# Six warm-up matmuls taken out of the tail of an attention and MLP kernel

## The chip, the cores and the metric

The kernel runs on one core of one Trainium2 chip. The metric is the device time of one execution in microseconds (us). All executions quoted were marked as fast, none as slow. The profiles give the span between the first and the last instruction, which is 1.7 to 1.9 us shorter than the device time in most runs.

A line of a profile gives the start, the length, the engine, the line of the kernel, the operation and its tiles; "x8" is the number of instructions merged in it, and the brackets give the idle time before it and what ended it. PE is TensorE's matmuls (and stands for TensorE in the recorded texts), PEld its weight loads, DVE VectorE, ACT ScalarE, POOL GpSimd. To evacuate a bank is to copy a finished result out of the accumulators; the kernel then sends the copy to memory.

## The reference, cut to what matters

The result is the sum of a normalized input's attention, a token-mixing MLP and the input itself:

```python
x = A_x                                   # [1, 2048, 512], bf16
xn = _layernorm(x, axis=-1)
return x + _A_ref(xn, A_wqkv, A_wo) + _B_ref(xn, B_w1, B_b1, B_w2, B_b2)
# _A_ref: 32 heads of 16, softmax over 2048 keys, heads joined, then "@ wo"
```

What matters here is the last step for the last quarter of the rows: all heads' results times `wo`, plus a part that has been computed earlier.

## The kernel before

The kernel is a program that lays out every instruction in order when it is built. Scores, exponentials and the products with V fill the first 675 us. The tail then projects the last heads for four tiles of 128 rows. `oT` holds the heads in four groups, T = 0 to 3. Groups 0 and 1 are long in the accumulators. Group 2 and a half of group 3 come from earlier blocks. The other half of group 3, `oL`, is what the very last block leaves, and VectorE has to normalize it first.

```python
def warm_up(n, bk, src=pT[:, NPB - 1, 0:512], keys=(("pT", NPB - 1),)):
    for _ in range(n):          # a result that nobody reads: keeps TensorE busy
        sc.add("pe", lambda e: e.matmul(bank(bk), lhsT=src[:, 0:128], rhs=src, start=True, stop=True),
               reads=keys, writes=[("bank", bk)], cost=("F", (0, 1, 2, 3), 0.3), name="warm")

def task_last():                # VectorE: normalize the last block
    ...                         # cut: views
    yield op(lambda e: e.transpose(denb[:, tb_, :], bank(PV_BANK)), ...)        # L1121
    yield op(lambda e: e.reciprocal(rcomp[:, 0, :], ...), ...)                  # L1123
    for half in range(2):
        yield op(lambda e, half=half: e.transpose(..., rl[:, :, half, :]...), ...)                          # L1127
        yield op(lambda e, half=half: e.tensor_tensor(v(oL, half), v(bank(PV_BANK), half), ..., ALU.mult),  # L1130
                 ..., [("oTl", half)], ...)

def tail():
    ...                         # cut: which banks
    def heads_of(Tm, sti):      # L1142: one 128x512 matmul for row tile sti
        ...
    for sti in range(4):
        heads_of(2, sti)
    warm_up(6, 2 * slots[1] + 1, wo_c[:, 0, :], wk)
    for sti in range(4):
        heads_of(3, sti)        # waits for L1095 on VectorE
    for half in range(2):       # L1155: eight matmuls, four on each half of oL
        for sti in (half, half + 2):
            for a in range(2):
                ...             # lhsT=oL[...half...], rhs=wo_t[...], reads ("oTl", half)
    for sti in (0, 2, 1, 3):    # evacuate: ScalarE for tile 3, VectorE for the others
        ...                     # L1162 (ScalarE), L1165 (VectorE), then one output transfer each
```

The softmax here doesn't subtract the row's maximum and nothing guards it: scores larger than these inputs give would overflow.

Of the kernel before, what the change touches and what calls it, by code (L numbers as in the profile page):

```python
# [359 lines left out]
def bass_parallel_sum__softmax_full_mha__mixer_token_mlp__prompt_kernel(  # L360
# [18 lines left out]
    with ExitStack() as es:  # L379
        block = es.enter_context(nc.Block())  # L380

        def sb(name, shape, dt):
            return es.enter_context(nc.sbuf_tensor(name, shape, dt))
# [14 lines left out]
        wo_c = sb("wo_c", [128, 4, D], BF16)  # L398
# [18 lines left out]
        def oT(qb):  # L417
            return oT_a[:, qb] if qb < 2 else oT_b[:, qb - 2]
# [23 lines left out]
        def bank(i):  # L442
            return ps[:, i * 512:(i + 1) * 512]
# [6 lines left out]
        def dma(q, dst, src, reads, writes, name="", noncontig=False, out_dma=False, cost=None):  # L450
            if noncontig:
                def fn(eng, dst=dst, src=src):
                    with nc.allow_non_contiguous_dma(reason="tiny strided vector load"):
                        return eng.dma_start(dst, src)
            else:
                def fn(eng, dst=dst, src=src):
                    return eng.dma_start(dst, src)
            return sc.add(q, fn, reads=reads, writes=writes, name=name, dma=True, out_dma=out_dma, cost=cost)
# [208 lines left out]
        def warm_up(n, bk, src=pT[:, NPB - 1, 0:512], keys=(("pT", NPB - 1),)):  # L667
            for _ in range(n):
                sc.add("pe", lambda e: e.matmul(bank(bk), lhsT=src[:, 0:128], rhs=src, start=True, stop=True),  # L669
                       reads=keys, writes=[("bank", bk)], cost=("F", (0, 1, 2, 3), 0.3), name="warm")  # L670
# [463 lines left out]
        def tail():  # L1134
            qb, T = NQB - 1, 3
            wk = [("wo_c", e_, r) for e_ in range(2) for r in range(4)]
            slots = sorted(range(3), key=lambda z: sc.ready("pe", [], [("bank", 2 * z), ("bank", 2 * z + 1)]))
            tbk = [2 * slots[0], 2 * slots[0] + 1, 2 * slots[1], EX_BANK]
            osl = [osb[:, 0, :], osb[:, 1, :], t_bf[:, 512:1024], t_bf[:, 1024:1536]]

            def heads_of(Tm, sti):
                sc.add("pe", lambda e: e.matmul(  # L1142
                    bank(tbk[sti]), lhsT=oT(qb)[:, Tm, 128 * sti:128 * (sti + 1)], rhs=wo_c[:, Tm, :],
                    start=Tm == 2 and sti < 3, stop=False),
                    reads=[("oTc", qb, 2) if Tm == 2 else ("oTh", sti // 2)] + wk, writes=[("bank", tbk[sti])])
            for sti in range(4):
                heads_of(2, sti)
            warm_up(6, 2 * slots[1] + 1, wo_c[:, 0, :], wk)
            for sti in range(4):
                heads_of(3, sti)  # L1150
            for half in range(2):
                for sti in (half, half + 2):
                    h = sti // 2
                    for a in range(2):
                        sc.add("pe", lambda e, sti=sti, h=h, a=a, half=half: e.matmul(  # L1155
                            bank(tbk[sti]), lhsT=oL[:, 256 * a + 128 * half:256 * a + 128 * half + 128],
                            rhs=wo_t[:, 2 * h + a, :], start=False, stop=a == 1),
                            reads=[("oTl", half)] + [("wo_t", c) for c in range(4)], writes=[("bank", tbk[sti])])
            for sti in (0, 2, 1, 3):
                st = 4 * qb + sti  # L1160
                if sti == 3:
                    sc.add("act", lambda e: e.activation(osl[3], bank(tbk[3]), ACTF.Identity),  # L1162
                           reads=[("bank", tbk[3])], writes=[("osl", 3)], cost=(0.5, 0.6))
                else:
                    sc.add("dve", lambda e, sti=sti: e.scalar_tensor_tensor(  # L1165
                        osl[sti], bank(tbk[sti]), 1.0, resid[:, sti, :], ALU.mult, ALU.add),
                        reads=[("bank", tbk[sti]), ("resid", sti)],
                        writes=[("osl", sti), ("osb", sti) if sti < 2 else ("osl2",)])
                dma("act" if sti == 3 else "sp", out2[128 * st:128 * (st + 1), :], osl[sti], reads=[("osl", sti)],
                    writes=[("out", st)], name="st_out", out_dma=True)  # L1170
# [467 lines left out]
        assert sorted(resid_done) == [0, 1, 2, 3]  # L1638
        load_lib(library_config.standard)
        tail()  # L1640
        if DEBUG_SCHED:
            print("modelled end", {e: round(sc.free[e], 1) for e in sc.free}, "busy", {e: round(v, 1) for e, v in sc.busy.items()},
# [54 lines left out]
```

## Time and profile before

| | before |
|---|---|
| time, median of the first 3 executions (6 in all) | 685.25 us (685.16 us) |
| span of the profiled execution | 683.2 us |
| last PV matmuls of the loop | to about 675.0 us |
| tail, from there to the end | 8 us |
| work of TensorE in the tail | 4 + 6 + 4 + 8 matmuls |

Everything that decides lies in the last 8 us, and the prediction below shows the lines. Three things have to be kept in mind in reading them. A matmul of 128x512 is recorded as 379 ns long, but the next one starts 216 ns after it (the six warm-ups of before, from 675.85 to 677.15). A VectorE instruction can start before the record of the one ahead of it ends: in the prediction's view L1127 starts at 677.02, 0.08 us before the end of L1130 (676.68 + 0.42). And a few matmul records are missing (the page of before counts 12975 matmuls and 12978 weight loads): a group shown as "x3" or "x7" can have had four or eight, and the number of weight loads tells.

### The profile page before, as it was taken

The page shows a single profiled execution, that of the slowest core. Times are in us where ns is not written, and L with a number is a line of the kernel's source. Part 1 is how long each engine was busy: PE and PEld are TensorE (multiplying, and loading weights), DVE is VectorE, ACT ScalarE, POOL GpSimd, SP SyncE. Part 2 cuts the span into 40 slices and gives each one's busy share as a digit, 9 for nine tenths or more (in the row PEclk, how much of TensorE's full clock was granted, in tenths as well). Part 3 has the DMA queues.
Part 4 walks back from the last instruction along what each step waited for, and adds up shares of the span by engine and source line. Part 5 has one row for each costly group of instructions (what it writes and reads, how often), then busy time and mean ns, then how long its engine had stood idle before and what let it go on. Part 6 is the DMA issues. An engine that isn't in the chain of part 4 may idle for free.

```text
span 683.2 us, 29532 instructions
## 1 busy us (share of the span) xinstructions
PE 671.5 (98%) x12975; PEld 312.9 (46%) x12978; DVE 617.0 (90%) x882; ACT 667.7 (98%) x731; POOL 416.7 (61%) x717
## 2 busy tenths in 40 slices
PE   8999999999999999999999999999999999999997
PEld 4534544445444455444444444444444444444443
DVE  7989899899998898999899899999999999989886
ACT  6999999999999999999999999999999999999995
POOL 5446557476576654667666677666657576565552
PEclk9999999999999999999999999999999999999999
DMA  7502100220002201122211112222221222212221
GB/s 216 132 8 52 24 15 23 51 48 24 19 18 49 49 22 20 26 49 47 49 38 27 41 44 58 53 57 47 46 59 35 59 55 56 54 45 66 46 50 46
DMA packets 86256, 32.85 MB, mean 48 GB/s; under 512 B 67440, under 2 KB 86128, under 8 KB 86128
## 3 DMA queue, kind: packets, MB, share of 16 engines
q1 hardware_dynamic: 85696, 30.58, 19.8%
q8 instruction: 101, 1.65, 1.0%
q10 hardware_dynamic: 432, 0.39, 0.2%
q14 instruction: 27, 0.22, 0.1%
HBM read 21.76 MB, written 2.35 MB: 35 GB/s over the span
## 4 chain that ended last, share of the span: by engine, by line
PE 73%; ACT 21%; DVE 3%; issue 1%; POOL 1%; DVEq 0%
PE ps L843 29%; PE ps L776 27%; PE ps L874 14%; ACT pT L800 14%; ACT x_sb L800 6%; PE ps L928 2%; ACT gT_sb L985 1%; DVE hx L588 1%; DVE pT L811 1%; POOL mv L584 0%; PE ps L669 0%; DVE x_sb L811 0%; PE ps L600 0%; PE ps L1155 0%; PE ps L1142 0%
## 5 line engine op out<-in xcount | busy, mean ns | idle before, releaser
L800 ACT ACTIVATE pT<-ps 128x1024 bf16<-128x1024 f32 x488 | 486.4, 1136 | 2.2 <-PE ps L776 1.7
L811 DVE TENSOR_SCALAR pT<-ps 128x1024 int16<-128x1024 f32 x220 | 269.2, 1224 | 26.2 <-PE ps L776 17.4
L776 PE MATMUL ps<-QT,KT 32*128 32x512 bf16 x2048 | 283.3, 384 | 5.3 <-ACT pT L800 3.2
L817 POOL INT64_ADD pT<-pT x342 | 206.5, 613 | 121.4 <-DVE pT L820 57.2
L843 PE MATMUL ps<-pT,V 128*32 128x256 bf16 x4696 | 242.1, 275 | 0.9 <-POOL pT L817 0.3
L800 ACT ACTIVATE x_sb<-ps 128x1024 bf16<-128x1024 f32 x223 | 241.7, 1142 | 0.2
L776 PEld LDWEIGHTS ps<-QT,KT 32*128 32x128 bf16 x2048 | 78.3, 91 | 179.7 <-ACT pT L800 66.9
L843 PEld LDWEIGHTS ps<-pT,V 128*32 128x32 bf16 x4696 | 111.7, 96 | 69.2 <-issue 55.3
L811 DVE TENSOR_SCALAR x_sb<-ps 128x1024 int16<-128x1024 f32 x93 | 113.7, 1222 | 9.7 <-PE ps L776 6.9
L817 POOL INT64_ADD pT<-x_sb x152 | 91.5, 612 | 48.8 <-DVE pT L820 28.8
L843 PE MATMUL ps<-x_sb,V 128*32 128x256 bf16 x1904 | 120.8, 275 | 0.0
L817 POOL INT64_ADD x_sb<-pT x120 | 73.1, 613 | 45.0 <-DVE pT L820 26.1
L843 PE MATMUL ps<-pT,VM 128*32 128x256 bf16 x920 | 63.7, 275 | 0.0
L820 DVE TENSOR_SCALAR pT<-pT 128x1024 int16<-128x1024 int16 x138 | 58.3, 425 | 3.9
L843 PEld LDWEIGHTS ps<-x_sb,V 128*32 128x32 bf16 x1904 | 49.5, 96 | 25.0 <-issue 20.8
L874 PE MATMUL ps<-gT_sb,wblk 128*32 128x512 bf16 (+1 forms) x704 | 57.9, 384 | 0.0
L874 PE MATMUL ps<-hx,wblk 128*32 128x512 bf16 x598 | 52.5, 383 | 0.1
L817 POOL INT64_ADD x_sb<-x_sb x44 | 26.9, 614 | 18.1 <-DVE pT L820 11.7
L882 PE MATMUL ps<-hx,wblk 32*128 32x512 bf16 (+1 forms) x92 | 35.5, 386 | 0.0
L843 PEld LDWEIGHTS ps<-pT,VM 128*32 128x32 bf16 x920 | 24.2, 96 | 12.8 <-issue 12.2
L820 DVE TENSOR_SCALAR pT<-x_sb 128x1024 int16<-128x1024 int16 x64 | 27.0, 425 | 1.9
L820 DVE TENSOR_SCALAR x_sb<-pT 128x1024 int16<-128x1024 int16 x60 | 25.6, 428 | 1.7
(107 smaller groups left out, 444.2 us busy)
## 6 DMA issues: line engine op xcount, KB each, us to landing
wblk<-in_B_w_dram SPq DMA_DIRECT2D x10, 512.0 KB, 4.3
wblk<-in_B_w_dram SPq DMA_DIRECT2D x16, 320.0 KB, 3.7
oC<-OT SPq DMA_DIRECT2D x248, 16.0 KB, 1.8
denb<-rden_scratch SPq DMA_DIRECT2D x124, 32.0 KB, 2.0
xr<-in_A_x_dram SPq DMA_DIRECT2D x16, 128.0 KB, 2.8
dcomp<-OT SPq DMA_DIRECT2D x124, 2.0 KB, 1.8
QT<-Qall SPq DMA_DIRECT2D x120, 16.0 KB, 1.8
out_dram<-osb SPq DMA_DIRECT2D x14, 128.0 KB, 1.9
```

Of the source, the lines that this page charges most:

```text
L588: return [dict(eng="dve", fn=lambda e: e.tensor_scalar(xn_sb[:, t, :], xn_sb[:, t, :], mv[:, t, 3:4], None, ALU.mult), reads=[("xn", t), ( ...
L776: specs.append(dict(eng="pe", fn=lambda e, r=r, bk=bk: e.matmul(bank(bk), lhsT=KT[32 * r:32 * r + 32, T, 128 * kt:128 * (kt + 1)], rhs=QT[ ...
L800: return [dict(eng="act", fn=lambda e: e.activation(buf(pbuf[n]), ps[:, s_ * 1024:(s_ + 1) * 1024], ACTF.Exp, scale=LN2_128), reads=[("ban ...
L811: return dict(eng="dve", fn=lambda e: e.tensor_scalar(buf_i(w), ps[:, s_ * 1024:(s_ + 1) * 1024], IBIAS, 0.0, ALU.add, ALU.max), reads=[(" ...
L817: return dict(eng=eng, fn=lambda e: e.int64_add(buf_i(o).bitcast(I64), buf_i(w).bitcast(I64), SHIFTS[k] * 0x0001000100010001), reads=[("pT ...
L820: return dict(eng=eng, fn=lambda e: e.tensor_scalar(buf_i(o), buf_i(w), float(SHIFTS[k]), 1.0, ALU.add, ALU.mult), reads=[("pT", w)], writ ...
L843: specs.append(dict(eng="pe", fn=lambda e, c=c, h=h, i=i, off=off: e.matmul(bank(PV_BANK)[32 * c:32 * c + 32, 256 * par:256 * par + 256], ...
L874: specs.append(dict(eng="pe", fn=lambda e, c=c, w=w: e.matmul(bank(EX_BANK)[32 * c:32 * c + w, :], lhsT=lhs_of(32 * c, 32 * c + w), rhs=rh ...
L882: return [dict(eng="pe", fn=lambda e: e.matmul(bank(EX_BANK)[0:dst_rows, :], lhsT=lhs_of(0, dst_rows)[rs], rhs=rhs[rs], start=begin, stop= ...
L928: return [dict(eng="pe", fn=lambda e, ct=ct, c=c: e.matmul(bank(EX_BANK)[32 * c:32 * c + 32, 128 * i:128 * (i + 1)], lhsT=xnT[:, ct, 128 * ...
L985: yield "act", [dict(eng="act", fn=lambda e, ap=ap: e.activation(ap, ap, ACTF.Gelu_apprx_tanh), reads=[("gT", f) for f in fts], writes=[(" ...
```

## The change

The intent: nobody reads the six warm-ups' results. They only keep TensorE busy while VectorE prepares the last heads; that this was meant to hold its clock is my reading of it. (In the profile of before the granted clock is 1.00 up to 682.0 us and 0.50 to 0.51 from there on, with TensorE's last matmul started at 679.52.) The four matmuls of group 3 can fill that wait as well, and they are needed anyway.

```diff
@@ -1145,7 +1145,6 @@
             for sti in range(4):
                 heads_of(2, sti)
-            warm_up(6, 2 * slots[1] + 1, wo_c[:, 0, :], wk)
             for sti in range(4):
                 heads_of(3, sti)
```

Lines below it are numbered one lower afterwards: L1155 becomes L1154, L1162 L1161 and L1165 L1164.

## The prediction

Cuts are marked in the text below: what they said of the hardware is not shown by any run of this case. No term of the sum is among them. The 0.216 us for each matmul is read from the six warm-ups in the profile of before, and the sum came to a gain of 0.80 to 0.84 us, taken as 0.81: 685.25 - 0.81 = 684.44 us. Step 3's 0.2155 us is 0.2158 us in that profile, (679.521 - 678.010) / 7, and the last start comes to 678.68 with either.

> **What bounds the kernel now.** I looked first at the page's summary, the engines' busy shares, to see whether six matmuls could matter at all.

> ```profile
> PE 671.5 (98%) x12975; PEld 312.9 (46%) x12978; DVE 617.0 (90%) x882; ACT 667.7 (98%) x731; POOL 416.7 (61%) x717
> ```

> TensorE and ScalarE are both busy for 98% of the span. But these are averages over 683.2 us, and the edited line runs once, in the last 8 us. Nothing ahead of it moves: the kernel is a list of instructions laid out in order when it is built, and the call that goes is the last part of that list but one. The banks of the tail are picked before it. So the whole question lies in the window from 674 us to the end, and its own limits decide. Second view: the chain of waits that ended last, for that window.

> ```profile
> 673.95 1.09 PE ps L843 x40
> 675.04 0.16 issue
> 675.20 0.81 PE ps L1142 x3
> 676.01 1.29 PE ps L669 x6
> 677.31 0.86 PE ps L1142 x4
> 678.17 1.74 PE ps L1155 x8
> 679.91 0.02 issue
> 679.94 0.60 ACT oT L1162
> ```

> The columns are start, length, and what ran. The six warm-up matmuls (L669) lie on the chain for 1.29 us, between the projection of the heads of T = 2 (L1142, first group) and that of T = 3 (L1142, second group), and the eight matmuls of the very last heads (L1155) close it. The first L1142 group shows three matmuls, where the code has four. Four weight loads are there, the first at 674.97, so I take the record of the first matmul as missing: it ran at about 674.98 and the "issue" of 0.16 us isn't a real wait. PE is then gapless from 674.98 to the start of the last matmul.

> On a chain does not yet mean worth its length. Third view: the timeline of VectorE in the same window, which makes what L1155 reads (columns: start, length, what; in brackets the idle time before it).

> ```profile
> 674.38 0.87 DVE L1095 TENSOR_TENSOR wkv_raw<-oC,denb 64x256 bf16<-64x256 f32 x2 [1.82 <-DMA oC<-OT]
> 675.17 0.70 DVE L1121 STREAM_TRANSPOSE denb<-ps 128x512 f32<-128x512 f32 x1
> 675.91 0.25 DVE L1123 RECIPROCAL rcomp<-denb 128x16 f32<-128x16 f32 x1
> 676.20 0.45 DVE L1127 STREAM_TRANSPOSE oC<-rcomp 128x256 f32<-128x256 f32 x1
> 676.68 0.42 DVE L1130 TENSOR_TENSOR oT<-ps,oC 128x256 bf16<-128x256 f32 x1
> 677.02 0.44 DVE L1127 STREAM_TRANSPOSE oC<-rcomp 128x256 f32<-128x256 f32 x1
> 677.49 0.43 DVE L1130 TENSOR_TENSOR oT<-ps,oC 128x256 bf16<-128x256 f32 x1
> 678.64 0.69 DVE L1165 SCALAR_TENSOR_TENSOR osb<-ps,hx 128x512 bf16<-128x512 f32 x1 [0.73 <-PE ps L1155]
> 679.25 0.68 DVE L1165 SCALAR_TENSOR_TENSOR oT<-ps,hx 128x512 bf16<-128x512 f32 x1
> 679.85 0.68 DVE L1165 SCALAR_TENSOR_TENSOR osb<-ps,hx 128x512 bf16<-128x512 f32 x1
> ```

> Three dates are in it. The heads of T = 3 (L1095) are whole at 675.25. The first half of the very last heads (first L1130) is ready at 676.68 + 0.42 = 677.10, the second half at 677.49 + 0.43 = 677.92. L1155 starts on the first half only at 678.01, some 0.9 us after it was ready, and VectorE then idles 0.73 us for PE. So the filler is longer than the wait that it fills, and PE is the late one here.

> [...]six warm-ups from 675.85 to 677.15 are 0.216 us each, though each is recorded as 379 ns long. The recorded length is therefore not what one matmul costs.[...]

> [...]In this trace the granted clock is 1.00 in every 0.5 us stretch up to 682.0 and 0.51 from 682.0 to 682.5, with the last matmul started at 679.52. The drop thus came some 2.1 us after PE had run out of work (679.9)[...], and it fell when nothing needed PE any more.

> **The change, part by part.** Removed: six 128x512 matmuls, 6 x 0.216 = 1.30 us of PE. Nothing is added, and no wait goes, since the bank that they wrote belongs to the slot whose other bank the projection takes anyway, and nobody read theirs.

> Moved, step by step:
> 1. The four matmuls of T = 2 end their issue at 675.85, as now. Those of T = 3 follow at once, because their data is whole at 675.25: they start at 675.85 instead of 677.15 and hold PE to 675.85 + 4 x 0.216 = 676.71.
> 2. L1155 then waits for the first half: ready at 677.10, plus the way from VectorE to PE. I read that from one case where PE stood idle for VectorE: the copy of the last but one block ends at 659.95 and the next weight load is at 660.01, so 0.06 us. The first matmul starts at about 677.17 instead of 678.01. PE is idle for 677.17 - 676.71 = 0.46 us. The gain on PE is 0.84 us, not 1.30.
> 3. Four matmuls on the first half run to 677.17 + 0.86 = 678.03. The second half is seen by PE at 677.92 + 0.06 = 677.98, so just in time. The last matmul starts at 677.17 + 7 x 0.2155 = 678.68 (now 679.52).
> 4. Evacuation on VectorE. From the start of a bank's last matmul to its evacuation it is now 678.64 - 678.23 = 0.41 us. The first bank is complete for it at 677.17 + 0.22 + 0.41 = 677.80, but VectorE works on the second L1130. From a TENSOR_TENSOR of this shape to the next instruction it is 677.02 - 676.68 = 0.34 us, so it is free at 677.83. VectorE is now the later one, by 0.03 us. Three evacuations at the present spacing of 0.605 us start at 677.83, 678.44 and 679.04 (their banks are complete at 677.80, 678.23 and 678.66). The last starts at 679.04 instead of 679.85: 0.81 us earlier.
> 5. Evacuation on ScalarE (L1162) follows the last matmul: 678.68 + 0.42 = 679.10 instead of 679.94: 0.84 us earlier.
> 6. Four output transfers follow at the same spacing as now, two of them issued last and together (680.56 now, from both queues), 1.8 to 2.1 us to land. They can only shift. The later of the two issues moves by 0.80 us.

> Sum: 0.80 to 0.84 us, limited by VectorE; I take 0.81. 685.25 - 0.81 = 684.44 us, 0.12% of the whole. Of the 1.30 us removed, 0.46 us turn into a wait for VectorE, and 0.03 us of the rest are lost to it at the evacuation.

> **The rivals.**
> - *The whole 1.30 us is gained* (683.95 us). The chain, taken at its word, says so. Against it stands the 677.10 of the first L1130: L1155 can't start before its operand exists.
> - *VectorE sets the end already, so nothing is gained* (685.2 us). For it: VectorE's line from 674.38 to 677.92 has no gap above 0.1 us, and its next work is the evacuation. Against: the 0.73 us in which it waits for L1155. This wait is the upper limit of what VectorE can give, together with the overlap of 0.08 us between two of its instructions, which is where the 0.81 comes from.
> - *The idle PE is throttled, which is what the filler was there to prevent.* If the last eight matmuls ran at half clock from 677.17, at 0.43 us each, the last would start at 680.18, 0.66 us later than now: about 685.9 us. For it: the clock does fall at the end of this very trace. Against: that took 2.1 us of idle time, and the new gap is 0.46 us behind a stretch that was full; in the loop, PE's weight loads wait hundreds of times for 0.2 to 0.4 us and the clock stays at 1.00. I give this 3%.
> - *A wait met with an empty PE queue costs more than 0.06 us.* [...]With 0.3 us the gain would be about 0.6 us (684.65 us). Each 0.1 us here, above the 0.03 us of slack in step 4, costs 0.1 us. This is the likeliest way to be off.
> - *The output transfers hide it.* No: each is issued by what its evacuation releases, 0.03 us after its end, and the first now starts at 679.36, behind everything else.

> **Range and chances.** The three runs of before lie within 0.16 us, so noise is of the order of 0.1 to 0.2 us. The mechanism leaves 0.55 to 0.9 us of gain. That gives 684.15 to 684.85 us for 8 times in 10, a little lopsided to the slow side because of the fourth rival. A change of 2% would be 13.7 us; the whole tail from the last attention block to the end is 8 us. No rival comes near, so "within 2%" is as good as certain, and the rest is for a run that is disturbed.

> **What would show it.** In the changed kernel's timeline: no L669 after the loop's own; the second L1142 group at about 675.85 in place of 677.15; an idle PE of about 0.46 us ahead of L1155 that ends by DVE oT L1130, and L1155 from about 677.17; no wait of 0.73 us ahead of the first L1165, which starts back to back with the second L1130 near 677.83; ScalarE's L1162 near 679.10; a span of about 682.4 us; granted clock 1.00 until PE is done. Wrong would be: L1155 starting later than 677.3 (the empty queue costs more), 0.43 us between matmuls (throttle), L1165 still waiting for PE by more than 0.1 us, or any shift ahead of 674 us larger than 0.1 us, which would mean that the two traces differ by something that I took as fixed.

## The result, and the profile after

The changed kernel takes 684.34 us (median of 6, 684.26 to 684.46) against 685.16 us before (median of 6, 685.07 to 685.25): 0.82 us less. The slowest run after is faster than the fastest before. The ratio is 0.9988, with a 95% interval from 0.9975 to 1.0001. Ratios here are the mean time of one kernel's fast runs over that of the other's of the same rounds, so not quite the ratio of the medians quoted. The predicted time was 684.44 us.

The order of instructions on the other four engines is the same in both kernels, and on TensorE it differs by the six matmuls alone. The page's first line after:

```profile
PE 670.7 (98%) x12969; PEld 312.4 (46%) x12972; DVE 617.0 (90%) x882; ACT 667.7 (98%) x731; POOL 417.6 (61%) x717
```

TensorE has six matmuls and six weight loads fewer. The timeline of VectorE after, to be laid beside that of before:

```profile
674.26 0.87 DVE L1095 TENSOR_TENSOR wkv_raw<-oC,denb 64x256 bf16<-64x256 f32 x2 [1.45 <-DMA oC<-OT]
675.36 0.72 DVE L1121 STREAM_TRANSPOSE denb<-ps 128x512 f32<-128x512 f32 x1 [0.23 <-PE ps L843]
...
676.88 0.42 DVE L1130 TENSOR_TENSOR oT<-ps,oC 128x256 bf16<-128x256 f32 x1
...
677.69 0.42 DVE L1130 TENSOR_TENSOR oT<-ps,oC 128x256 bf16<-128x256 f32 x1
678.03 0.68 DVE L1164 SCALAR_TENSOR_TENSOR osb<-ps,hx 128x512 bf16<-128x512 f32 x1
678.63 0.68 DVE L1164 SCALAR_TENSOR_TENSOR oT<-ps,hx 128x512 bf16<-128x512 f32 x1
679.23 0.68 DVE L1164 SCALAR_TENSOR_TENSOR osb<-ps,hx 128x512 bf16<-128x512 f32 x1
```

The wait of 0.73 us ahead of the first evacuation is gone. VectorE goes from the second L1130 straight to it, 678.03 - 677.69 = 0.34 us later. ScalarE's evacuation after:

```profile
679.30 0.60 ACT L1161 ACTIVATE oT<-ps 128x512 bf16<-128x512 f32 x1 [4.55 <-PE ps L1154]
```

The weight loads and matmuls of TensorE in the same stretch (two views of the same kernel, the weight loads first):

```profile
675.24 1.41 PEld L1142 LDWEIGHTS ps<-wo_c,wkv_raw 128*128 128x128 bf16 x8 [0.21 <-issue]
677.36 0.55 PEld L1154 LDWEIGHTS ps<-wo_t,oT 128*128 128x128 bf16 x4 [0.71 <-DVE oT L1130]
678.17 0.60 PEld L1154 LDWEIGHTS ps<-wo_t,oT 128*128 128x128 bf16 x4 [0.27 <-DVE oT L1130]
```

```profile
675.47 1.67 PE L1142 MATMUL ps<-wo_c,wkv_raw 128*128 128x512 bf16 x7 [0.16 <-issue]
677.36 1.90 PE L1154 MATMUL ps<-wo_t,oT 128*128 128x512 bf16 x8 [0.22 <-DVE oT L1130]
```

All eight L1142 run in one stretch, and the array then waits for VectorE. The wait that the view shows, 0.22 us, starts at the recorded end of the last L1142 (675.47 + 1.67 = 677.14). Counted from when the array could have taken the next matmul it is longer: the first L1142 ran at about 675.25, eight of them take 8 x 0.216 = 1.73 us, and from 676.98 to 677.36 it is 0.38 us. It differs between executions: counted in the same way, it is 0.56 us in `n0` below, which is the same kernel.

The two profiles can't be subtracted as they stand. The execution after runs late from the start: already at 102 us a given VectorE instruction (L811) is at 102.37 instead of 102.11, and it keeps this 0.26 us to the tail. So the tails are compared from a mark of their own. From the start of L1121 to the start of the last evacuation on VectorE it was 679.85 - 675.17 = 4.68 us and is 679.23 - 675.36 = 3.87 us: 0.81 us less. This quantity, "VectorE's path", is used below. It leaves out the offset, but not all of the jitter: L1121 starts 0.12 to 0.34 us after TensorE's first weight load of the tail, depending on the execution, and where TensorE sets the end, a late L1121 makes the path look shorter.

### The profile page after: what moved, and what is told of

The parts are those of the page before. It is cut to its first block, busy times and chain, and to the rows that moved or that the text cites. A ratio compares the mean times of both kernels' runs of the same rounds, so it can differ in the third digit from the quotient of the medians.

```text
span 682.6 us, 29520 instructions
## 1 busy us (share of the span) xinstructions
PE 670.7 (98%) x12969; PEld 312.4 (46%) x12972; DVE 617.0 (90%) x882; ACT 667.7 (98%) x731; POOL 417.6 (61%) x717
## 4 chain that ended last, share of the span: by engine, by line
PE 74%; ACT 21%; DVE 3%; issue 1%; POOL 1%; DVEq 0%
PE ps L843 29%; PE ps L776 27%; PE ps L874 14%; ACT pT L800 14%; ACT x_sb L800 6%; PE ps L928 2%; PE ps L669 1%; ACT gT_sb L985 1%; DVE hx L588 1%; DVE pT L811 1%; POOL mv L584 0%; PE ps L600 0%; DVE x_sb L811 0%; PE ps L613 0%; PE ps L882 0%
## 5 line engine op out<-in xcount | busy, mean ns | idle before, releaser
L811 DVE TENSOR_SCALAR pT<-ps 128x1024 int16<-128x1024 f32 x220 | 269.1, 1223 | 26.4 <-PE ps L776 17.6
L843 PE MATMUL ps<-pT,V 128*32 128x256 bf16 x4696 | 242.1, 275 | 0.9 <-POOL pT L817 0.3
L843 PEld LDWEIGHTS ps<-pT,V 128*32 128x32 bf16 x4696 | 111.6, 96 | 69.2 <-issue 55.3
L811 DVE TENSOR_SCALAR x_sb<-ps 128x1024 int16<-128x1024 f32 x93 | 113.6, 1222 | 9.8 <-PE ps L776 6.9
L843 PE MATMUL ps<-x_sb,V 128*32 128x256 bf16 x1904 | 120.8, 275 | 0.0
L843 PE MATMUL ps<-pT,VM 128*32 128x256 bf16 x920 | 63.7, 275 | 0.0
L843 PEld LDWEIGHTS ps<-x_sb,V 128*32 128x32 bf16 x1904 | 49.5, 96 | 25.0 <-issue 20.8
L843 PEld LDWEIGHTS ps<-pT,VM 128*32 128x32 bf16 x920 | 24.2, 96 | 12.9 <-issue 12.2
```

Of the source, the lines that this page charges most:

```text
L811: return dict(eng="dve", fn=lambda e: e.tensor_scalar(buf_i(w), ps[:, s_ * 1024:(s_ + 1) * 1024], IBIAS, 0.0, ALU.add, ALU.max), reads=[(" ...
L843: specs.append(dict(eng="pe", fn=lambda e, c=c, h=h, i=i, off=off: e.matmul(bank(PV_BANK)[32 * c:32 * c + 32, 256 * par:256 * par + 256], ...
```

## The experiments

All changes are made to the changed kernel. Four kernels ran in each group, on one chip with shared runs of the kernel before, 5 rounds each. The before median was 685.20 us in the first two groups and 685.25 us in the third.

**First group: how many warm-ups, and where.** `n0` is the changed kernel again. `n2` and `n4` put 2 and 4 of the six back where they stood. `n10` (run with the second group) has ten. `end6` has all six, but behind the last matmul.

```diff
             for sti in range(4):
                 heads_of(2, sti)
+            warm_up(2, 2 * slots[1] + 1, wo_c[:, 0, :], wk)      # n2; 4 in n4, 10 in n10
             for sti in range(4):
                 heads_of(3, sti)
             ...
+            warm_up(6, 2 * slots[1] + 1, wo_c[:, 0, :], wk)      # end6 instead: after L1154
```

> The changed kernel again, on the chip of the next three. My theory (PE was late by 0.84 us, VectorE's data is the floor): 0.80 us faster than before, 0.7 to 0.95. Rival A (the whole filler was on the path): 1.3 us faster. Rival B (noise only): 0.0 to 0.2.

> Two of the six warm-ups kept. My theory: the idle gap of 0.46 us ahead of the last heads holds 2 x 0.216 = 0.43 us, so it is filled and nothing is lost: the same as n0 within 0.06 us, 0.80 us faster than before. Rival A (each warm-up costs its 0.216 us): 0.43 us slower than n0, and 0.87 us faster than before.

> Four kept. My theory: two more than fit in the gap, so 0.43 us later on PE and, with 0.03 us of slack, about 0.40 us slower than n0 and 0.40 to 0.43 us faster than before; ahead of the first evacuation VectorE waits about 0.3 us for PE. Rival A says the same 0.43 us faster than before, but then n2 is at 0.87 and n0 at 1.30.

> Ten warm-ups, four more than before. My theory: beyond what fits in the gap each costs its whole 0.216 us: 0.86 us slower than before. Rival B (noise only): within 0.2 us of before.

> All six warm-ups back, but behind the last matmul, where only the outputs' evacuation and transfer are left. My theory (their place costs, not their number): as n0 within 0.06 us, 0.80 us faster than before. Rival C (the shorter instruction stream or its layout is what pays): as before, 0.0 us.

| warm-ups | time, median (lowest to highest), us | against before, us | VectorE's path, us |
|---|---|---|---|
| 0 (`n0`) | 684.35 (684.34 to 684.48) | -0.85 | 3.85 |
| 2 (`n2`) | 684.53 (684.43 to 684.63) | -0.67 | 3.85 |
| 4 (`n4`) | 684.74 (684.53 to 684.90) | -0.46 | 4.32 |
| 6 (before) | 685.20 | 0 | 4.68 |
| 10 (`n10`) | 686.04 (685.93 to 686.40) | +0.84 | 5.62 |
| 6 at the end (`end6`) | 684.38 (684.12 to 684.50) | -0.82 | 3.86 |

VectorE's path stays flat from 0 to 2 warm-ups and then climbs by about 0.2 us for each, which is one matmul. Counted from TensorE's own first weight load of the tail to the last evacuation, the steps are even: 4.44 us in `n4`, 4.88 us before and 5.74 us in `n10`, so 0.22 us for each warm-up. `end6` has as many instructions as before and is as fast as `n0`, so rival C (the shorter stream pays) falls: the place costs, not the number. Rival A (each warm-up costs its length) falls with `n2`, which would have had to be 0.43 us slower than `n0`.

`n2` is a partial miss all the same. I expected at most 0.06 us against `n0`; the medians differ by 0.18 us and the ranges hardly overlap. The profiled tails are alike, with equal paths of 3.85 us, and the 0.10 us by which the profiled `n2` is later at L1121 (675.55 against 675.45) is to 0.07 us there at 102 us already (102.34 against 102.27), long before any warm-up of the tail. The cause of the rest stays open. The pair `d3` and `d3_fill9` below shows a difference of the same size and sign.

The first evacuation in `n4`, in VectorE's timeline:

```profile
678.44 0.69 DVE L1165 SCALAR_TENSOR_TENSOR osb<-ps,hx 128x512 bf16<-128x512 f32 x1 [0.36 <-PE ps L1155]
```

The wait for TensorE is back at half its size: 0.36 us where before had 0.73 us.

**Second group: what bounds the tail now.** The prediction says that after the change two paths end together, TensorE to ScalarE, and VectorE. Three kernels with wrong results take away one or both. `pe_free` lets the last matmuls read weights that were loaded long ago, so TensorE never waits. `dve_short` leaves out VectorE's second half. `both` does both. They ran on another chip than `n0`, with the same median of before.

```diff
-  bank(tbk[sti]), lhsT=oL[:, 256 * a + 128 * half:256 * a + 128 * half + 128],
+  bank(tbk[sti]), lhsT=wo_c[:, 0, 256 * a + 128 * half:256 * a + 128 * half + 128],   # pe_free, both
+  bank(tbk[sti]), lhsT=oL[:, 256 * a:256 * a + 128],                                  # dve_short
-  reads=[("oTl", half)] + ...
+  reads=wk + ...                # pe_free, both        ("oTl", 0) in dve_short
-            for half in range(2):
+            for half in range(1):                       # in task_last: dve_short, both
```

> Wrong result on purpose: the last eight matmuls take their weights from a tile that was loaded long ago instead of from the last heads, so PE has no wait of 0.46 us. My theory says that the evacuation on VectorE is as late as PE (0.03 us of slack), so PE's wait is worth nothing alone: 0.80 us faster than before, like n0, within 0.1 us. Rival D (the gap on PE is the loss that is left): 0.46 us faster than n0, about 1.25 us faster than before.

> Wrong result on purpose: VectorE's work on the second half of the last heads is left out, 0.81 us of it, and the matmuls read the first half twice. My theory: PE still waits for the first half, so the last matmul and the ScalarE evacuation behind it do not move: like n0 within 0.1 us, 0.80 us faster than before; the first evacuation on VectorE moves by only 0.03 us. Rival E (VectorE alone sets the end): up to 0.5 us faster than n0.

> Both edits together, wrong result on purpose. My theory of two paths that end together: only now the end moves, by 0.46 us (PE's wait) against n0, so 1.25 us faster than before, 1.1 to 1.4. Rival D expects the same as pe_free, rival E the same as dve_short.

| | time, median (lowest to highest), us | against before, us | VectorE's path, us |
|---|---|---|---|
| `n0` (first group) | 684.35 (684.34 to 684.48) | -0.85 | 3.85 |
| `pe_free` | 684.20 (684.02 to 684.32) | -1.00 | 3.87 |
| `dve_short` | 684.34 (684.17 to 684.49) | -0.86 | 3.84 |
| `both` | 683.85 (683.76 to 683.94) | -1.35 | 3.45 |

First VectorE of `dve_short`, then VectorE of `both`; each fence has the last instruction on the first half and the first and last evacuation:

```profile
677.02 0.42 DVE L1130 TENSOR_TENSOR oT<-ps,oC 128x256 bf16<-128x256 f32 x1
678.15 0.69 DVE L1164 SCALAR_TENSOR_TENSOR osb<-ps,hx 128x512 bf16<-128x512 f32 x1 [0.70 <-PE ps L1154]
...
679.35 0.68 DVE L1164 SCALAR_TENSOR_TENSOR osb<-ps,hx 128x512 bf16<-128x512 f32 x1
```

```profile
676.73 0.42 DVE L1130 TENSOR_TENSOR oT<-ps,oC 128x256 bf16<-128x256 f32 x1
677.46 0.69 DVE L1164 SCALAR_TENSOR_TENSOR osb<-ps,hx 128x512 bf16<-128x512 f32 x1 [0.30 <-PE ps L1154]
...
678.66 0.68 DVE L1164 SCALAR_TENSOR_TENSOR osb<-ps,hx 128x512 bf16<-128x512 f32 x1
```

With 0.81 us of its work gone, VectorE in `dve_short` waits 0.70 us for TensorE and gains next to nothing on its path: 3.84 us against 3.87 and 3.85 us in two profiles of the changed kernel. That is as small as the slack of 0.03 us that the prediction worked out, but too small to be told from the difference between those two. With TensorE freed as well, the path falls by 0.42 us. So neither path is the bound alone: rival E (VectorE alone) falls with `dve_short`, rival D (the gap on TensorE is the loss left) would want 0.46 us from `pe_free`. There TensorE indeed waits for nothing ahead of the last eight matmuls (no bracket):

```profile
676.98 1.89 PE L1154 MATMUL ps<-wo_t,wo_c 128*128 128x512 bf16 x8
```

`pe_free` gained 0.15 us more than `n0`, where I had allowed 0.1. VectorE's path is the same. But ScalarE's evacuation no longer ends with VectorE's last one: ScalarE issues its transfer at 679.53 and the sync engine its last at 679.94, whereas after the change they come at 679.93 and 679.94. Each moves 128 KB. ScalarE's transfer, the only one that took 2.1 us to land in the changed kernel, took 1.9 us here. In `d7` below, where the two are issued at 686.62 and 686.26, it took 1.7 us; in `n0`, `dve_short` and `both`, where they are issued within 0.01 us, 2.1 us. Whether the two disturb each other was not shown.

**Third group: what the warm-ups were for.** Does TensorE's clock fall in a longer gap? `d3` and `d7` do VectorE's first transpose four and eight times over instead of once, with the same result. `d3_fill9` and `d7_fill20` fill the longer wait with warm-ups at the old place.

```diff
-            yield op(lambda e: e.transpose(denb[:, tb_, :], bank(PV_BANK)), ...)
+            for _ in range(4):                          # 8 in d7 and d7_fill20
+                yield op(lambda e: e.transpose(denb[:, tb_, :], bank(PV_BANK)), ...)
...
+            warm_up(9, 2 * slots[1] + 1, wo_c[:, 0, :], wk)      # d3_fill9; 20 in d7_fill20
```

> No warm-ups, and VectorE's first transpose of the tail is done four times instead of once (same result), to make PE's wait longer: 3 x about 0.62 us, so 1.86 us more. My theory: PE idle for 0.46 + 1.86 = 2.3 us, which this chip's clock survives (the trace of before kept the full clock for 2.1 us after the last matmul): 1.86 us slower than n0, so 1.05 us slower than before, and the same as d3_fill9 within 0.1 us. Rival F (any idle of PE is throttled): last eight matmuls 0.43 us apart, up to 1.7 us slower than d3_fill9.

> As d3, with nine warm-ups, 1.94 us, which fit in the gap of 2.3 us. My theory: as d3 within 0.1 us, 1.05 us slower than before.

> No warm-ups, the transpose eight times: 7 x 0.62 = 4.34 us more, PE idle for about 4.8 us. Theory of the clock[...]: the last eight matmuls run at 0.43 us apart, in all or in most executions, and the kernel is 0.9 to 1.7 us slower than d7_fill20; granted clock 0.5 in that stretch. Rival G (the clock never matters in a tail this short): as d7_fill20 within 0.1 us, 3.5 us slower than before.

> As d7, with twenty warm-ups, 4.32 us, which fit in the gap of 4.8 us and keep PE busy. Both theories: clock 1.00, 0.216 us between matmuls, 4.34 us slower than n0, so 3.5 us slower than before.

| | gap on TensorE, us | every execution, us |
|---|---|---|
| `d3` | 2.6 | 686.31, 688.03, 686.47, 686.18, 687.97 |
| `d3_fill9` | 0.7 | 686.38, 686.67, 686.52, 686.44, 686.66 |
| `d7` | 5.8 | 690.75, 690.83, 690.87, 691.27 |
| `d7_fill20` | 1.4 | 689.62, 690.18, 689.51, 689.38, 689.45 |

Of `d7` four executions came back. The gaps are those of the profiled execution, counted as above, from 0.216 us after the start of the last matmul ahead of the gap. A repeated transpose cost 0.75 us (four took 2.97 us) and not the 0.62 us that I had assumed: the repeats start 0.75 us apart, each just after the record of the one before (0.72 us) has ended, and each writes the tile that the one before wrote. All four kernels are therefore longer than the absolute figures that I gave; the pairs still compare.

`d7` is 1.34 us slower than `d7_fill20` by the medians, and its profile shows why. Weight loads of the last eight matmuls in `d7`, and then the stretches around them (columns: stretch, length, busy time and number of instructions for PE, PEld, DVE, ACT and POOL, granted clock, DMA share, GB/s):

```profile
682.76 0.13 PEld L1155 LDWEIGHTS ps<-wo_t,oT 128*128 128x128 bf16 x2 [6.09 <-DVE oT L1131]
683.17 0.15 PEld L1155 LDWEIGHTS ps<-wo_t,oT 128*128 128x128 bf16 x1 [0.28 <-issue]
683.60 0.15 PEld L1155 LDWEIGHTS ps<-wo_t,oT 128*128 128x128 bf16 x1 [0.28 <-issue]
```

```profile
681.50:682.00 0.50, 0.00 (x0) 0.00 (x0) 0.45 (x2) 0.00 (x0) 0.00 (x0) 1.00 0.00 0
682.00:682.50 0.50, 0.00 (x0) 0.00 (x0) 0.47 (x2) 0.00 (x0) 0.00 (x0) 0.50 0.00 0
```

The loads come every 0.43 us, twice the usual 0.216, and the granted clock fell from 1.00 to 0.50 at 682.0. The eight matmuls take 3.19 us, in `d7_fill20` 1.90 us at a clock of 1.00:

```profile
682.76 3.19 PE L1155 MATMUL ps<-wo_t,oT 128*128 128x512 bf16 x8 [5.60 <-DVE oT L1131]
```

```profile
682.44 1.90 PE L1156 MATMUL ps<-wo_t,oT 128*128 128x512 bf16 x8 [1.21 <-DVE oT L1131]
```

Rival G (the clock never matters in such a tail) falls. In `d3` I had expected the clock to survive. In three of five executions it seems to; two are about 1.7 us slower than the median of those three, where `d7` lost 1.34 us. No profile fell on one of those two, so that they are the clock is argued and not shown. The profiled `d3` ran its eight matmuls at full clock:

```profile
679.30 1.90 PE L1155 MATMUL ps<-wo_t,oT 128*128 128x512 bf16 x8 [2.47 <-DVE oT L1131]
```

The mean clock of each execution doesn't decide it: 0.998 in the slow two, 0.997 to 1.000 in the others. Three things speak for the clock. `d3_fill9` has no such execution in five. The size fits: with `d7`'s figures, eight matmuls wholly at half clock start the last one 7 x 0.21 us later, and from a bank's last matmul to its evacuation `d7` took 0.67 us (683.17 to 683.84) instead of 0.41, so I estimate 1.7 us. And the frequency fits an estimate from the clock records.

Rival F (any idle of TensorE is throttled) falls with the changed kernel itself, which idles for 0.38 us at a clock of 1.00, and with the profiled `d3`, which idles for 2.6 us at 1.00.

The runs point to no correct kernel that beats both: `n0` is the changed kernel, `end6` does the same with useless work behind it, and `pe_free` and `both`, which are faster, compute something else.

## Why the prediction was right, point by point

1. *Group 3 follows at once.* Right: eight L1142 run without a break.
2. *The wait for the first half.* Right in kind. Data was ready at 676.88 + 0.42 = 677.30 and TensorE started at 677.36: 0.06 us, the predicted figure. The fourth rival (a wait with an empty queue costs more) has nothing to show: it is 0.06 us in `d3` (679.24 to 679.30) and `d7` (682.70 to 682.76) too, after much longer waits. The gap came out as 0.38 us and not 0.46 us, because in the profile of before L1095 came late after its transfer and held L1121 up. L1121 started 0.20 us after the first weight load of the tail there, and 0.12 us after it in the changed kernel (675.36 - 675.24).
3. *The second half is just in time.* Right: ready at 677.69 + 0.42 = 678.11, its weight load at 678.17, while the four matmuls ahead of it hold TensorE until 677.36 + 0.86 = 678.22.
4. *VectorE becomes the later one by 0.03 us, and the last evacuation moves by 0.81 us.* Right: 4.68 to 3.87 us on VectorE's path, and from the first bank's matmuls the evacuation could have started at 677.36 + 0.22 + 0.41 = 677.99, where VectorE was free at 678.03.
5. *ScalarE follows the last matmul by 0.42 us.* Right: the last matmul starts at 677.36 + 7 x 0.216 = 678.87, L1161 at 679.30.
6. *The transfers only shift.* Right: the last two are issued at 679.94 and 679.93, 0.60 us after the second-last as before, and land with the same medians, 1.7 to 2.1 us (the prediction says 1.8 to 2.1, but one of before's took 1.7 us).

That the time came within 0.1 us of 684.44 is partly luck. The sum rests on one execution of before, in which L1121 started 0.20 us after TensorE's first weight load. With the 0.12 to 0.34 us that the other traces show, the same sum gives a gain between 0.89 and 0.67 us, still inside the stated range.

Two of the prediction's own signs of being wrong came up by the letter: L1154 (then L1155) started later than 677.3, and the shift ahead of 674 us is larger than 0.1 us. Both come from the 0.26 us by which that execution ran late from the start, which the prediction had not allowed for; the span is 682.6 us and not 682.4 for the same reason. From the start of L1121 to the first matmul on the last heads it is 677.36 - 675.36 = 2.00 us, as predicted (677.17 - 675.17).

Of the rivals, "the whole 1.30 us" fell with the result and with `n2`; "VectorE sets the end already" fell with the result, and came true as the limit of the gain; the clock does fall in `d7`, to 0.50 in a gap of 5.8 us, but stayed at 1.00 in the 0.38 us that this change opens. The chances were right for the reason given: a tail of 8 us can't move 685 us by 2%.

What the prediction said too firmly is that the drop of the clock comes some 2.1 us after TensorE runs out of work. That was one observation, counted from the recorded end of the last matmul (2.3 us from the end of its issue). The fourteen traces range from 2.3 to 5.2 us, a spread of less than one step of 3.413 us; `d3`, which it led me to expect at full clock, probably is not always.

## What to carry to other kernels

Filler on an engine is free only as far as it fits into the wait that it fills: here two warm-ups left VectorE's path at 3.85 us, and four made it 4.32 us. Read when the awaited data is ready on the producing engine, compare it with when the consumer starts, and cut the filler to that; real work that only waits behind the filler is the best filler there is. When a wait has been cut, look for the path that now ends together with it: here one more gain needed two changes at once. And keep filler where a gap would otherwise exceed about 2 us, since the earliest fall of the clock seen here came 2.3 us after the last matmul's issue. Each matmul of filler too many costs its 0.22 us (`n4` to `n10`); too little filler cost half the clock in `d7`, for 3.4 us.
